# Sums of token blocks for the last two groups: operands read from PSUM on VectorE, and the places of their splits

## The chip, the cores and the metric

One core of a Trainium2 chip runs the whole program. The metric is the device time of one execution in microseconds; before the change it was 810.95 us, the median of 3 runs (809.65 to 811.36).

## The reference

Eight batches of 576 tokens pass through an attention layer (8 heads of width 64; heads 0 to 3 see a local window of 32 positions, heads 4 to 7 a stride of 32) and then through a mixer layer. All is float32:

```python
scores = np.where(masks[None], scale * np.matmul(q, k.transpose(0, 1, 3, 2)), -1e9)
x = softmax(scores) @ v                       # as [batch, 576, 512]
h = np.maximum(xt @ w_tok1, 0.0) @ w_tok2     # xt = x transposed to [batch, 512, 576]
u = x + h.transpose(0, 2, 1)
h2 = np.maximum(u @ w_ch1, 0.0) @ w_ch2       # w_ch1 512 x 1536, w_ch2 1536 x 512
return u + h2
```

The change lies in the last step, `u @ w_ch1`, for the last 1024 of the 4608 tokens.

## The kernel before

**Numbers.** Every float32 operand of a large product is held as two parts, a high part rounded to the format that TensorE multiplies (`fp32r`) and a low part, the rest: `uh`/`ul`, `w1h`/`w1l`, `gh`/`gl`. A product is three matmuls (high·high, high·low, low·high). A *split* makes the two parts of a tile: a copy on ScalarE (ACT) gives the high part, a subtraction on VectorE (DVE) the low one.

**Groups.** The 4608 tokens form nine groups of 512 (`GT`), 0 to 8. `u` of a group is eight tiles of 128 x 512, high and low for four blocks `cc` of 128 channels. A batch's 576 tokens fill the rest of one group and a part of the next: `tok2` (L483) makes them, first the 64 tokens of batch 7 that end group 7 (a narrow call), then the 512 tokens that are group 8. It transposes `x` into a PSUM tile `pu`, adds `h·w_tok2` there, copies `uh` from it on ACT (L516) and subtracts on DVE (L517). It is called for two `cc` at a time, and its two PSUM tiles come from a pool `ps_t` of two banks.

**Groups 0 to 6** go through `mlp` (L909). It walks over 12 blocks of 128 hidden channels: an up product (L921), ReLU and split (L926, L927), a down product that adds to four accumulators (`down`, L712). Between these are numbered slots, four to a block, into which other work is put by hand with `at(slot, function)`. All engines follow the order in which the program is written (`manual_schedule`), so an instruction that waits holds everything behind it on its own engine. In group 6 (L1099 to L1113) slots 35 and 36 hold the two narrow calls for batch 7, slots 37 and 39 the two calls that make group 8. Slot 38 lies inside the down product of block 9, slots 39 and 40 directly behind it; then come the down products of blocks 10 and 11, 24 matmuls.

**Groups 7 and 8** go together through `last_two` (L794), which replaces the eight block products of a 2 x 2 by 2 x 2 product by seven (Strassen's scheme as Winograd wrote it). The weights are taken as 2 x 2 blocks of 128 x 256, the tokens as two halves of channels by two groups. With `b1` = group 7 and `b2` = group 8, four sums of token blocks are needed, each of two tiles of 128 x 512 and each split:

- t1 = b2[0:2] − b1[0:2]
- t2 = b2[2:4] − t1
- t3 = b2[2:4] − b2[0:2]
- t4 = b1[2:4] − t2

`token_sums` (L748) makes them as a generator whose parts are run at slots 38 and 40 and then three times in the first iteration of `last_two`. `chain` (L722) applies one operation after the other to one output tile. Since `b1` and `b2` are read as high and low parts, t1 takes three operations a tile, t2 two, t3 three (on GpSimd, POOL), t4 two (one tile on DVE, one on POOL). The tile `third` that holds t3 has the name `sw`, of which there is one buffer.

`weight_sums(i)` (L731) makes the four sums of weight blocks s1 to s4 of iteration `i`: ten operations of 128 x 256 on POOL into the tile `sw`, then four splits (L743 on ACT, L744 on DVE) into tiles `sh`, `sl`. Those of iterations 0 and 1 are made in group 6.

**The loop of `last_two`** has six iterations of two hidden blocks. `times` (L802) is one of the seven products, six matmuls. The order of iteration 0 on TensorE (PE) is a11·b11, a12·b21, s1·t1, s2·t2, s4·b22, s3·t3. The order of a later iteration is s1·t1, a11·b11, then a22·t4 of the iteration before (`last_product`), a down product of 12 matmuls, s4·b22, s2·t2, a down product, s3·t3, a12·b21. `kept` (L820) copies a PSUM tile to SBUF on ACT; `plus` (L825) adds a PSUM tile and an SBUF tile on DVE; `relu` (L805, L806) is ReLU with a split.

- The product s2·t2 adds to the bank `a` of a11·b11, and so waits until `kept(a)` has copied it (`p1`).
- The product s3·t3 adds to the same bank, and so waits until `kept(a)` has copied it again (`p16`).
- The first product of iteration i + 1 writes the bank `h0`, and so waits until `c12 = plus(b, p16)` has read it.

`result` (L705) adds `u` to an accumulator (L708 on DVE; for group 6 L709 on POOL) and stores it. For group 6 blocks 0 and 1 are done behind the last down product, blocks 2 and 3 at the end of iteration 0.

Of the kernel before, what the change touches and what calls it, by code (L numbers as in the profile page):

```python
# [10 lines left out]
F32 = mybir.dt.float32  # L11
# [12 lines left out]
DM = H * D  # L24
# [83 lines left out]
def attn_mixer_kernel(ctx, tc, qT, kT, vw, qs, ks, vs, qsT, ksT, vsP, mask, words, outT):  # L108
# [374 lines left out]
    def tok2(ps_t, x_t, h, us, b, tail, ccs, whole_t2=None):  # L483

        t0, t1 = _span(b, tail)
        n, g0 = t1 - t0, 0 if tail else 64 * b
        o = 0 if t0 else 64
        chunks = [*([] if t0 else [NSC - 1]), *range(max(t0 - 64, 0) // P, (t1 - 64) // P)]
        pus = [ps_t.tile() for _ in ccs]
        for pu, cc in zip(pus, ccs):  # L490
            cs = slice(P * cc, P * cc + P)
            for k, c in enumerate(chunks):
                ps_t.matmul(pu[:, P * k:P * k + P], x_t[:, c, cs], ident,
                                 is_transpose=True, start=(k == 0), stop=False, skip_group_check=True)
        narrow = whole_t2 is None and n <= NARROW
        for pu, cc in zip(pus, ccs):
            cs = slice(P * cc, P * cc + P)
            if narrow:
                sides = pu[:, o:o + 2 * n].rearrange("p (k n) -> p k n", k=2)
            pu = pu[:, o:o + n]  # L500
            for m in range(2):
                if whole_t2 is not None:
                    terms = ((pu, h[m], whole_t2[:, m]),)
                else:
                    hh, hl = h[m]
                    th, tl, both = t2h[:, m, t0:t1], t2l[:, m, t0:t1], t2[:, m, :, t0:t1]
# [221 lines left out]

    combos = {}

    def weight_sums(i):  # L731

        a11, a12, a21, a22 = ([w[:, 2 * c:2 * c + 2, P * f:P * f + P].bitcast(F32) for w in (w1h, w1l)] for f in (2 * i, 2 * i + 1) for c in range(2))
        whole = pools["fin"].tile([P, 4, 2, P], F32, name="sw")
        s1, s2, s3, s4 = (whole[:, k] for k in range(4))
        chain(nc.gpsimd, s1, a21[0], (ALU.add, a22[0]), (ALU.add, a21[1]), (ALU.add, a22[1]))
        chain(nc.gpsimd, s2, s1, (ALU.subtract, a11[0]), (ALU.subtract, a11[1]))
        chain(nc.gpsimd, s3, a11[0], (ALU.subtract, a21[0]), (ALU.add, a11[1]), (ALU.subtract, a21[1]))
        chain(nc.gpsimd, s4, a12[0], (ALU.subtract, s2), (ALU.add, a12[1]))
        yield  # L740
        sh, sl = (pools["fin"].tile([P, 4, 2, P], F32R, name="s" + k, bufs=2) for k in "hl")
        for k in range(4):
            nc.scalar.copy(out=sh[:, k], in_=whole[:, k])  # L743
            nc.vector.tensor_tensor(out=sl[:, k], in0=whole[:, k], in1=sh[:, k].bitcast(F32), op=ALU.subtract)  # L744
        combos[i] = [(sh[:, k], sl[:, k]) for k in range(4)]
        yield

    def token_sums():  # L748

        def f(pair):  # L750
            return [t.bitcast(F32) for t in pair]

        b1, b2 = us[NG - 2], us[NG - 1]
        t1 = [const.tile([P, NSC, DT], F32R, name="t1" + k).rearrange("p c n -> p (c n)")[:, :2 * GT].rearrange("p (c n) -> p c n", c=2) for k in "hl"]
        wholes = []
        for c in range(2):
            x, y = f(b2[c]), f(b1[c])
            w = xp.tile([P, GT], F32, name="xh")
            chain(nc.vector, w, x[0], (ALU.subtract, y[0]), (ALU.add, x[1]), (ALU.subtract, y[1]))
            wholes.append(w)  # L760
        todo = [split_u(w, t1[0][:, c], t1[1][:, c]) for c, w in enumerate(wholes)]
        yield
        for g in todo:
            g()
        t2 = xp.tile([P, NSC, DM], F32R, name="x", bufs=1).rearrange("p c n -> p (c n)")[:, :4 * GT].rearrange("p (k c n) -> p k c n", k=2, c=2)
        twos = []
        for c in range(2):
            x = f(b2[2 + c])
            w = xp.tile([P, GT], F32, name="xlo")
            chain(nc.vector, w, x[0], (ALU.subtract, wholes[c]), (ALU.add, x[1]))  # L770
            twos.append(w)
        third = pools["fin"].tile([P, 4, 2, P], F32, name="sw").rearrange("p (c k) m n -> p c (k m n)", c=2)
        for c in range(2):
            x, y = f(b2[2 + c]), f(b2[c])
            chain(nc.gpsimd, third[:, c], x[0], (ALU.subtract, y[0]), (ALU.add, x[1]), (ALU.subtract, y[1]))
        for g in [split_u(w, t2[:, 0, c], t2[:, 1, c]) for c, w in enumerate(twos)]:
            g()
        t3 = [[xp.tile([P, DM], F32R, name=f"h{k}{m}", bufs=1) for m in range(2)] for k in "hl"]
        t4 = const.tile([P, 2, 2, S], F32R, name="t2").rearrange("p c k n -> p (c k n)")[:, :4 * GT].rearrange("p (k c n) -> p k c n", k=2, c=2)
# [6 lines left out]
        for c in range(2):  # L786
            x = f(b1[2 + c])
            chain((nc.vector, nc.gpsimd)[c], twos[c], x[0], (ALU.subtract, twos[c]), (ALU.add, x[1]))
        yield
        for g in [split_u(w, t4[:, 0, c], t4[:, 1, c]) for c, w in enumerate(twos)]:  # L790
            g()
        yield

    def last_two():  # L794
# [45 lines left out]
        for i in range(NFC // 2):  # L840
# [5 lines left out]
            if i:  # L846
# [2 lines left out]
                times(a, a11, b11, True)  # L849
                p5, p1 = kept(b), kept(a)  # L850
                last_product(i - 1, before)
                down_all(fe - 2)
                times(b, s4, b22, False)
                times(a, s2, t2, False)
            else:
                times(a, a11, b11, True)
                p1 = kept(a, "gh")
                times(c, a12, b21, True)
                t1, t2, t3, t4 = combos["t"]
                times(b, s1, t1, True)  # L860
# [5 lines left out]
            c12 = plus(b, p16)  # L866
            if i:
                down_all(fo - 2)
            else:
                next(combos["token"])  # L870
            if i:
                next(sums, None)
                sums = weight_sums(i + 2) if i + 2 < NFC // 2 else iter(())
                next(sums, None)
            times(a, s3, t3, False)
            later[fo] = plus(a, p5)
            if i:
                times(c, a12, b21, True)
            else:
                next(combos["token"])  # L880
            hidden[fe] = relu(plus(c, p1, None if i else "gl"), *new_g())
            later[fe] = relu(flat(c12), *in_place(fe))
            if i == 0:
                sums = weight_sums(2)
                next(sums)
                while left:
                    left.pop(0)()
            combos["a22"], before = a22, a
# [93 lines left out]
    def do_tok2(b, tail, ccs=range(NCC)):  # L982
        g = b + tail
        if g not in us:
            us[g] = new_u(pools["fin"] if g == NG - 1 else up if g % 2 else xp)
        tok2(ps_t, state["x"], state["h"], us[g], b, tail, ccs, None if b else t2e)

    def opened(name, **how):
        closing[name] = tc.tile_pool(name=name, reuse_waits="tile", **how)
# [86 lines left out]
    for g in range(NG - 2):  # L1076
# [10 lines left out]
        if b < B:  # L1087
# [11 lines left out]
            if b == B - 1:  # L1099
                at(21, attention_ends)  # L1100
                made["sums"] = []
                for i, k in ((21, 0), (26, 0), (26, 1), (31, 1)):
                    at(i, lambda i=i, k=k: (made["sums"].append(weight_sums(k)) if len(made["sums"]) == k else None, next(made["sums"][k])))
                for i, t in enumerate((37, 39)):
                    at(t, lambda i=i: do_tok2(b, True, (2 * i, 2 * i + 1)))

                def token_begins():
                    combos["token"] = token_sums()
                    next(combos["token"])

# [144 lines left out]
```

## Time and profile before

| | us |
|---|---|
| median of 3 runs (lowest, highest) | 810.95 (809.65, 811.36) |
| the profiled execution | 811.38 |
| its span in the profile | 809.6 |
| TensorE busy | 783.3 |
| VectorE busy | 530.4 |
| GpSimd busy | 319.7 |
| ScalarE busy | 259.8 |

The profile is of one execution; times in it count from the start of its span. PE is TensorE's matmuls, DVE VectorE, ACT ScalarE, POOL GpSimd. A busy time says how long instructions ran, not that the engine worked at its best: the duration of a matmul counts from its start to the end of its results, while the next one starts before that. The granted clock is a share of TensorE's full speed of 2.4 GHz; 0.5 is its lower level of 1.2 GHz. In a timeline a row gives start, duration, engine, line, operation, output and inputs, and how many were merged; brackets hold the engine's idle time ahead of it and what ended that.

### The profile page before, as it was taken

What the parts mean: (1) busy time and instruction counts of PE and PEld (TensorE: products, weight loads), DVE (VectorE), ACT (ScalarE), POOL (GpSimd) and SP (SyncE); (2) the same over time, 40 slices, a digit from 0 to 9 for tenths busy, and PEclk for the clock granted to TensorE, in tenths of its full rate; (3) what the DMA queues carried; (4) which work ended last, traced back from release to release, by engine and by line L of the source; (5) the groups of instructions that cost most, each with busy time, mean ns of one, the idle gap of its engine ahead of it and who ended that gap; (6) DMA issues with size and microseconds to landing.
All of it is one profiled execution on the core that took longest, in us unless ns stands there. A gap on an engine that the chain in (4) does not pass through costs nothing.

```text
span 809.6 us, 16277 instructions
## 1 busy us (share of the span) xinstructions
PE 783.3 (97%) x6284; PEld 639.7 (79%) x6284; DVE 530.4 (66%) x1810; ACT 259.8 (32%) x611; POOL 319.7 (39%) x330
## 2 busy tenths in 40 slices
PE   6799999999999999999999999999999998899997
PEld 5567778888888878888888888888888886688886
DVE  4687985556467777766767678677786459654340
ACT  6577873233222222222212222222121322333300
POOL 2300000043105782279127932685267607853000
PEclk9899999999999999999999999999999999999999
DMA  9547782245504250335033321434021200000011
GB/s 355 177 135 247 239 270 72 92 153 157 145 1 161 76 148 3 111 101 152 23 109 103 94 82 40 128 89 130 7 77 48 57 1 27 26 1 1 0 66 39
DMA packets 61545, 79.82 MB, mean 99 GB/s; under 512 B 16316, under 2 KB 46908, under 8 KB 61468
## 3 DMA queue, kind: packets, MB, share of 16 engines
q1 hardware_dynamic: 60044, 74.32, 29.6%
q0 software_dynamic: 1136, 4.06, 1.4%
q8 instruction: 49, 0.80, 0.4%
q10 hardware_dynamic: 288, 0.40, 0.1%
q14 instruction: 28, 0.23, 0.1%
HBM read 60.16 MB, written 18.48 MB: 97 GB/s over the span
## 4 chain that ended last, share of the span: by engine, by line
PE 84%; DVE 7%; ACT 4%; DMA 3%; issue 1%; SPq 0%; ACTq 0%; DVEq 0%
PE acc L716 29%; PE h L921 25%; PE t L82 19%; PE t L802 3%; PE h L802 2%; PE h L716 2%; PE t L716 2%; DVE xlo L726 1%; ACT as L185 1%; PE t L85 1%; DMA x<-xs 1%; DMA ek<-in_ksT 1%; ACT w_raw L138 1%; PE h L85 1%; DMA mask_sb<-in_mask 1%
## 5 line engine op out<-in xcount | busy, mean ns | idle before, releaser
L414 POOL TENSOR_TENSOR sprod<-sv,ss 128x512 f32<-128x512 f32 (+9 forms) x150 | 136.2, 951 | 122.1 <-issue 52.5
L366 POOL TENSOR_TENSOR sprod<-sk,sq 128x512 f32<-128x512 f32 x80 | 102.2, 1307 | 136.7 <-DVE ss L367 97.2
L716 PE MATMUL acc<-gh,w2h 128*128 128x512 f32 x384 | 152.3, 397 | 0.5 <-ACT gh L805 0.5
L716 PE MATMUL acc<-gl,w2h 128*128 128x512 f32 x384 | 150.4, 392 | 0.2 <-DVE gl L806 0.2
L716 PE MATMUL acc<-gh,w2l 128*128 128x512 f32 x384 | 150.4, 392 | 0.0
L921 PE MATMUL h<-uh,w1h 128*128 128x512 f32 x336 | 134.5, 400 | 2.1 <-DVE ul L517 1.4
L921 PE MATMUL h<-uh,w1l 128*128 128x512 f32 x336 | 131.3, 391 | 0.0
L921 PE MATMUL h<-ul,w1h 128*128 128x512 f32 x336 | 131.0, 390 | 0.0
L927 DVE SCALAR_TENSOR_TENSOR gl<-h,gh 128x512 fp32r<-128x512 f32 x84 | 57.8, 688 | 59.6 <-ACT gh L926 59.4
L926 ACT ACTIVATE gh<-h 128x512 fp32r<-128x512 f32 x84 | 50.5, 601 | 111.2 <-PE h L921 111.2
L416 DVE TENSOR_REDUCE so<-sprod 128x64 f32<-128x512 f32 (+9 forms) x150 | 73.9, 526 | 17.8 <-POOL sprod L414 17.7
L716 PEld LDWEIGHTS acc<-gh,w2l 128*128 128x128 f32 x384 | 72.5, 189 | 15.6
L716 PEld LDWEIGHTS acc<-gh,w2h 128*128 128x128 f32 x384 | 72.4, 189 | 15.4 <-ACT gh L805 1.0
L716 PEld LDWEIGHTS acc<-gl,w2h 128*128 128x128 f32 x384 | 72.6, 189 | 14.7 <-DVE gl L806 0.5
L185 ACT ACTIVATE as<-as,am 128x64 f32<-128x64 f32 x216 | 55.8, 337 | 67.4 <-DVE am L182 67.4
L921 PEld LDWEIGHTS h<-uh,w1h 128*128 128x128 f32 x336 | 63.1, 188 | 16.8 <-DVE ul L517 2.2
L921 PEld LDWEIGHTS h<-uh,w1l 128*128 128x128 f32 x336 | 63.1, 188 | 13.6
L921 PEld LDWEIGHTS h<-ul,w1h 128*128 128x128 f32 x336 | 63.2, 188 | 12.0
L182 DVE CUSTOM_DVE_ANT_0 as<-t,mask_sb 128x64 f32<-128x64 f32 x216 | 34.1, 220 | 33.0 <-PE t L82 26.8
L367 DVE TENSOR_REDUCE ss<-sprod 128x8 f32<-128x512 f32 x80 | 51.2, 670 | 6.2 <-POOL sprod L366 6.0
L517 DVE TENSOR_TENSOR ul<-t,uh 128x512 fp32r<-128x512 f32 (+5 forms) x44 | 22.9, 526 | 39.8 <-ACT uh L516 39.7
L82 PE MATMUL t<-t,hh 128*128 128x384 f32 (+5 forms) x184 | 47.9, 342 | 0.0
(198 smaller groups left out, 1238.7 us busy)
## 6 DMA issues: line engine op xcount, KB each, us to landing
w_raw<-in_words SPq DMA_DIRECT2D x21, 512.0 KB
lv<-in_vw SPq DMA_DIRECT2D x18, 390.0 KB
out_t<-xh SPq DMA_DIRECT2D x20, 256.0 KB
out_t<-xlo SPq DMA_DIRECT2D x16, 256.0 KB
lk<-in_kT SPq DMA_DIRECT2D x18, 208.0 KB
x<-xl SPq DMA_DIRECT2D x14, 256.0 KB
lq<-in_qT SPq DMA_DIRECT2D x18, 192.0 KB
xl<-ax SPq DMA_DIRECT2D x18, 192.0 KB
```

Of the source, the lines that this page charges most:

```text
L82: self.tc.stamp_issue_order_token(self.tc.nc.tensor.matmul(*args, **how).ins, self.pool.name)
L182: nc.vector.tensor_tensor_reduce(out=s_t[:, c, j, :], in0=sc[j].of[:, 64 * c:64 * c + 64], in1=mask_sb[:, m, :], scale=-SCALE, scalar=TOP, ...
L185: nc.scalar.activation(out=s_t[:, c, j, :], in_=s_t[:, c, j, :], func=AF.Exp, bias=m_t[:, c, j:j + 1], scale=-1.0)
L366: nc.gpsimd.tensor_tensor(out=pr, in0=k_t[:, n0:n0 + n], in1=q_t[:, i:i + 1].to_broadcast([P, n, D]), op=ALU.mult)
L367: return [lambda: nc.vector.tensor_reduce(out=s_t[:, i, n0:n0 + n], in_=pr, axis=AX.X, op=ALU.add)]
L414: nc.gpsimd.tensor_tensor(out=pr, in0=v_t[:, d0:d1, :n], in1=s_t[:, n - 1:n, :n].to_broadcast([P, d1 - d0, n]), op=ALU.mult)
L416: todo.append(lambda n=n, d0=d0, d1=d1, pr=pr: nc.vector.tensor_reduce(out=o_t[:, n - 1, d0:d1], in_=pr, axis=AX.X, op=ALU.add))
L716: nc.tensor.matmul(acc[cc], l[:, fc, cs], r, start=(fc == 0 and k == 0), stop=(fc == NFC - 1 and k == 2))
L802: nc.tensor.matmul(bank, a[x][:, c], b[c][y], start=start and c == 0 and k == 0, stop=(c == 1 and k == 2), skip_group_check=True)
L921: nc.tensor.matmul(ph, l[:, cc, fs], r, start=(cc == 0 and k == 0), stop=(cc == NCC - 1 and k == 2))
L926: nc.scalar.activation(out=gh, in_=ph, func=AF.Relu)
L927: nc.vector.scalar_tensor_tensor(out=gl, in0=ph, scalar=0.0, in1=gh.bitcast(F32), op0=ALU.max, op1=ALU.subtract)
```

## The change

1. `token_sums` begins at slot 36, with four new additions on POOL, high + low of each of the four tiles of group 7, into `wholes`. `tok2` returns its PSUM tiles, and `token_sums` takes them: behind the call at slot 37 it makes t1 as `pus - wholes` (one operation a tile), behind the call at slot 39 t2 as `pus - t1` (one) and t3 as `pus - b2h - b2l` (two), all on DVE. Slot 38 has t1's low parts, slot 40 those of t2 and then t4 as `wholes - t2` (one operation a tile, on DVE).
2. In iteration 0 the split of t3 follows the copy `p1`, and that of t4 the copy `p5`; nothing of `token_sums` comes later.
3. `weight_sums(2)` no longer runs on POOL from the end of iteration 0 on; it is made as a whole in iteration 1, behind `last_product(0)`, with its ten operations on DVE and its splits right behind them. `weight_sums(3)` and later ones stay on POOL, where they were.

```diff
-    def weight_sums(i):
+    def weight_sums(i, engine=nc.gpsimd):
...
-        chain(nc.gpsimd, s1, a21[0], (ALU.add, a22[0]), (ALU.add, a21[1]), (ALU.add, a22[1]))
+        chain(engine, s1, a21[0], (ALU.add, a22[0]), (ALU.add, a21[1]), (ALU.add, a22[1]))
...
     def token_sums():
-        b1, b2 = us[NG - 2], us[NG - 1]
+        b1 = us[NG - 2]
+        wholes = []
+        for c in range(NCC):
+            wholes.append(xp.tile([P, GT], F32, name="xh" if c < 2 else "xlo"))
+            nc.gpsimd.tensor_tensor(out=wholes[c], in0=b1[c][0].bitcast(F32), in1=b1[c][1].bitcast(F32), op=ALU.add)
+        pus = yield
+        b2 = us[NG - 1]
...
-        wholes = []
         for c in range(2):
-            x, y = f(b2[c]), f(b1[c])
-            w = xp.tile([P, GT], F32, name="xh")
-            chain(nc.vector, w, x[0], (ALU.subtract, y[0]), (ALU.add, x[1]), (ALU.subtract, y[1]))
-            wholes.append(w)
-        todo = [split_u(w, t1[0][:, c], t1[1][:, c]) for c, w in enumerate(wholes)]
+            nc.vector.tensor_tensor(out=wholes[c], in0=pus[c], in1=wholes[c], op=ALU.subtract)
+        todo = [split_u(wholes[c], t1[0][:, c], t1[1][:, c]) for c in range(2)]
         yield
         for g in todo:
             g()
+        pus = yield
...
-            chain(nc.vector, w, x[0], (ALU.subtract, wholes[c]), (ALU.add, x[1]))
...
-            chain(nc.gpsimd, third[:, c], x[0], (ALU.subtract, y[0]), (ALU.add, x[1]), (ALU.subtract, y[1]))
+            nc.vector.tensor_tensor(out=wholes[c], in0=pus[c], in1=wholes[c], op=ALU.subtract)
+        for c in range(2):
+            chain(nc.vector, third[:, c], pus[c], (ALU.subtract, b2[c][0]), (ALU.subtract, b2[c][1]))
+        todo = [split_u(wholes[c], t2[:, 0, c], t2[:, 1, c]) for c in range(2)]
+        yield
+        for g in todo:
+            g()
+        for c in range(2):
+            nc.vector.tensor_tensor(out=wholes[2 + c], in0=wholes[2 + c], in1=wholes[c], op=ALU.subtract)
...
-        for c in range(2):
-            x = f(b1[2 + c])
-            chain((nc.vector, nc.gpsimd)[c], twos[c], x[0], (ALU.subtract, twos[c]), (ALU.add, x[1]))
-        yield
-        for g in [split_u(w, t4[:, 0, c], t4[:, 1, c]) for c, w in enumerate(twos)]:
+        for g in [split_u(wholes[2 + c], t4[:, 0, c], t4[:, 1, c]) for c in range(2)]:
             g()
         yield
...
                 last_product(i - 1, before)
+                if i == 1:
+                    for _ in weight_sums(2, nc.vector):
+                        pass
                 down_all(fe - 2)
...
                 times(a, a11, b11, True)
                 p1 = kept(a, "gh")
+                next(combos["token"])
                 times(c, a12, b21, True)
...
                 down_all(fo - 2)
-            else:
-                next(combos["token"])
-            if i:
-                next(sums, None)
+                if i > 1:
+                    next(sums, None)
                 sums = weight_sums(i + 2) if i + 2 < NFC // 2 else iter(())
                 next(sums, None)
             times(a, s3, t3, False)
...
             if i:
                 times(c, a12, b21, True)
-            else:
-                next(combos["token"])
...
             if i == 0:
-                sums = weight_sums(2)
-                next(sums)
                 while left:
                     left.pop(0)()
...
-                for i, t in enumerate((37, 39)):
-                    at(t, lambda i=i: do_tok2(b, True, (2 * i, 2 * i + 1)))
...
-                at(38, token_begins)
-                for t in (40,):
-                    at(t, lambda: next(combos["token"]))
+                at(36, token_begins)
+                for i, t in enumerate((37, 39)):
+                    at(t, lambda i=i: combos["token"].send(do_tok2(b, True, (2 * i, 2 * i + 1))))
+                    at(t + 1, lambda: next(combos["token"]))
```

## Rows read from the trace of the kernel before

**Rows 1.** The page's head and its part 1: busy time, share of span, instructions.

```profile
span 809.6 us, 16277 instructions
...
PE 783.3 (97%) x6284; PEld 639.7 (79%) x6284; DVE 530.4 (66%) x1810; ACT 259.8 (32%) x611; POOL 319.7 (39%) x330
```

**Rows 2.** Windows: length, busy time and count of each engine, granted clock, DMA share, GB/s.

```profile
650.00:673.72 23.72, 23.64 (x124) 19.75 (x123) 13.52 (x24) 5.96 (x13) 4.20 (x3) 1.00 0.00 1
673.72:710.10 36.38, 30.75 (x121) 23.12 (x120) 28.49 (x32) 12.13 (x24) 29.63 (x28) 0.95 0.08 30
693.81:697.84 4.03, 4.03 (x12) 3.23 (x12) 3.72 (x5) 1.72 (x4) 3.79 (x5) 0.63 0.00 0
710.10:780.00 69.90, 69.90 (x310) 57.91 (x309) 29.33 (x46) 19.28 (x40) 17.77 (x23) 1.00 0.00 1
```

**Rows 3.** Timeline of PE: start, duration, what; its idle time before in brackets.

```profile
664.67 1.03 PE L82 MATMUL t<-ident,x 128*128 128x128 f32 x8
...
668.05 0.39 PE L82 MATMUL t<-t,hl 128*128 128x512 f32 x1
...
673.72 0.39 PE L802 MATMUL t<-uh,w1h 128*128 128x512 f32 x1
...
677.57 0.39 PE L802 MATMUL h<-t1h,sl 128*128 128x512 f32 x1
680.87 0.73 PE L802 MATMUL t<-x,sh 128*128 128x512 f32 x2 [2.91 <-ACT gh L820]
```

**Rows 4.** Waits of PE from 650 us on: total us, times, longest.

```profile
PE t L802 <- ACT gh L820: 2.9, 1, 2.9
PE t L802 <- DVE t L720: 1.0, 2, 0.8
```

**Rows 5.** Chain that ended last, in order of time: start, us, what.

```profile
700.74 2.72 PE acc L716 x12
```

**Rows 6.** Timeline of DVE, 655 to 703 us.

```profile
655.46 0.22 DVE L517 TENSOR_TENSOR ul<-xlo,uh 128x64 fp32r<-128x64 f32 x1 [0.31 <-ACT uh L516]
...
662.76 0.69 DVE L517 TENSOR_TENSOR ul<-t,uh 128x512 fp32r<-128x512 f32 x1 [0.67 <-ACT uh L516]
...
664.68 1.42 DVE L726 TENSOR_TENSOR xh<-xh,ul 128x512 f32<-128x512 f32 x2
...
669.32 1.29 DVE L517 TENSOR_TENSOR ul<-t,uh 128x512 fp32r<-128x512 f32 x2 [1.17 <-ACT uh L516]
...
674.64 1.66 DVE L726 TENSOR_TENSOR xlo<-xlo,ul 128x512 f32<-128x512 f32 x1
...
682.17 3.11 DVE L720 TENSOR_TENSOR hl<-sw,hh 128x512 fp32r<-128x512 f32 x2
685.21 0.68 DVE L825 TENSOR_TENSOR ul<-h,uh 128x512 f32<-128x512 f32 x1
...
693.67 1.22 DVE L806 SCALAR_TENSOR_TENSOR w1l<-ul,w1h 128x512 fp32r<-128x512 f32 x1
...
702.01 1.42 DVE L744 TENSOR_TENSOR sl<-sw,sh 128x256 fp32r<-128x256 f32 x4
```

**Rows 7.** Timeline of ACT.

```profile
679.71 0.62 ACT L719 CAST x<-xlo 128x512 fp32r<-128x512 f32 x1 [2.69 <-DVE xlo L726]
...
701.26 1.33 ACT L743 CAST sh<-sw 128x256 fp32r<-128x256 f32 x4
```

**Rows 8.** Timeline of POOL.

```profile
681.74 3.00 POOL L709 TENSOR_TENSOR xh<-xh,ul 128x512 f32<-128x512 f32 x2 [2.60 <-DVE xh L708]
684.70 1.73 POOL L726 TENSOR_TENSOR xlo<-uh,xlo 128x512 f32<-128x512 f32 x1
...
698.09 2.53 POOL L709 TENSOR_TENSOR xh<-xh,ul 128x512 f32<-128x512 f32 x2
703.51 0.74 POOL L726 TENSOR_TENSOR sw<-w1h 128x256 f32<-128x256 f32 x1 [2.89 <-DVE sl L744]
```

**Rows 9.** Window of the first two stores of group 6: same columns as rows 2.

```profile
683.06:687.00 3.94, 3.39 (x15) 2.29 (x14) 3.91 (x4) 0.09 (x1) 3.86 (x3) 1.00 0.35 133
```

More of the change, by code (lines that the diff above doesn't have):

```diff
@@ L517, in tok2 @@
             nc.vector.tensor_tensor(out=ul, in0=whole, in1=uh.bitcast(F32), op=ALU.subtract)
+        return pus
     closing = {"late": tc.tile_pool(name="late", bufs=1, side="right")}
@@ L735, in weight_sums @@
         s1, s2, s3, s4 = (whole[:, k] for k in range(4))
-        chain(nc.gpsimd, s1, a21[0], (ALU.add, a22[0]), (ALU.add, a21[1]), (ALU.add, a22[1]))
-        chain(nc.gpsimd, s2, s1, (ALU.subtract, a11[0]), (ALU.subtract, a11[1]))
-        chain(nc.gpsimd, s3, a11[0], (ALU.subtract, a21[0]), (ALU.add, a11[1]), (ALU.subtract, a21[1]))
-        chain(nc.gpsimd, s4, a12[0], (ALU.subtract, s2), (ALU.add, a12[1]))
+        chain(engine, s1, a21[0], (ALU.add, a22[0]), (ALU.add, a21[1]), (ALU.add, a22[1]))
+        chain(engine, s2, s1, (ALU.subtract, a11[0]), (ALU.subtract, a11[1]))
+        chain(engine, s3, a11[0], (ALU.subtract, a21[0]), (ALU.add, a11[1]), (ALU.subtract, a21[1]))
+        chain(engine, s4, a12[0], (ALU.subtract, s2), (ALU.add, a12[1]))
         yield
@@ L748, in token_sums @@
     def token_sums():
-        def f(pair):
-            return [t.bitcast(F32) for t in pair]
-        b1, b2 = us[NG - 2], us[NG - 1]
+        b1 = us[NG - 2]
[5 more added lines that the diff above has]
+        b2 = us[NG - 1]
         t1 = [const.tile([P, NSC, DT], F32R, name="t1" + k).rearrange("p c n -> p (c n)")[:, :2 * GT].rearrange("p (c n) -> p c n", c=2) for k in "hl"]
-        wholes = []
         for c in range(2):
-            x, y = f(b2[c]), f(b1[c])
-            w = xp.tile([P, GT], F32, name="xh")
-            chain(nc.vector, w, x[0], (ALU.subtract, y[0]), (ALU.add, x[1]), (ALU.subtract, y[1]))
-            wholes.append(w)
-        todo = [split_u(w, t1[0][:, c], t1[1][:, c]) for c, w in enumerate(wholes)]
+            nc.vector.tensor_tensor(out=wholes[c], in0=pus[c], in1=wholes[c], op=ALU.subtract)
+        todo = [split_u(wholes[c], t1[0][:, c], t1[1][:, c]) for c in range(2)]
         yield
@@ L764, in token_sums @@
             g()
+        pus = yield
         t2 = xp.tile([P, NSC, DM], F32R, name="x", bufs=1).rearrange("p c n -> p (c n)")[:, :4 * GT].rearrange("p (k c n) -> p k c n", k=2, c=2)
-        twos = []
-        for c in range(2):
-            x = f(b2[2 + c])
-            w = xp.tile([P, GT], F32, name="xlo")
-            chain(nc.vector, w, x[0], (ALU.subtract, wholes[c]), (ALU.add, x[1]))
-            twos.append(w)
+        t3 = [[xp.tile([P, DM], F32R, name=f"h{k}{m}", bufs=1) for m in range(2)] for k in "hl"]
+        t4 = const.tile([P, 2, 2, S], F32R, name="t2").rearrange("p c k n -> p (c k n)")[:, :4 * GT].rearrange("p (k c n) -> p k c n", k=2, c=2)
         third = pools["fin"].tile([P, 4, 2, P], F32, name="sw").rearrange("p (c k) m n -> p c (k m n)", c=2)
         for c in range(2):
-            x, y = f(b2[2 + c]), f(b2[c])
-            chain(nc.gpsimd, third[:, c], x[0], (ALU.subtract, y[0]), (ALU.add, x[1]), (ALU.subtract, y[1]))
-        for g in [split_u(w, t2[:, 0, c], t2[:, 1, c]) for c, w in enumerate(twos)]:
-            g()
-        t3 = [[xp.tile([P, DM], F32R, name=f"h{k}{m}", bufs=1) for m in range(2)] for k in "hl"]
-        t4 = const.tile([P, 2, 2, S], F32R, name="t2").rearrange("p c k n -> p (c k n)")[:, :4 * GT].rearrange("p (k c n) -> p k c n", k=2, c=2)
+            nc.vector.tensor_tensor(out=wholes[c], in0=pus[c], in1=wholes[c], op=ALU.subtract)
[4 more added lines that the diff above has]
+        for g in todo:
+            g()
+        for c in range(2):
+            nc.vector.tensor_tensor(out=wholes[2 + c], in0=wholes[2 + c], in1=wholes[c], op=ALU.subtract)
         combos["t"] = [[(h[:, c], l[:, c]) for c in range(2)] for h, l in (t1, (t2[:, 0], t2[:, 1]))]
@@ L785, in token_sums @@
         yield
-        for c in range(2):
-            x = f(b1[2 + c])
-            chain((nc.vector, nc.gpsimd)[c], twos[c], x[0], (ALU.subtract, twos[c]), (ALU.add, x[1]))
-        yield
-        for g in [split_u(w, t4[:, 0, c], t4[:, 1, c]) for c, w in enumerate(twos)]:
+        for g in [split_u(wholes[2 + c], t4[:, 0, c], t4[:, 1, c]) for c in range(2)]:
             g()
@@ L985, in do_tok2 @@
             us[g] = new_u(pools["fin"] if g == NG - 1 else up if g % 2 else xp)
-        tok2(ps_t, state["x"], state["h"], us[g], b, tail, ccs, None if b else t2e)
+        return tok2(ps_t, state["x"], state["h"], us[g], b, tail, ccs, None if b else t2e)
     def opened(name, **how):
```

## The prediction, made before the changed kernel was run

> **What bounds the kernel now.** The page first: TensorE is busy 783.3 of 809.6 us [rows 1], so only its gaps can be won. The windows say where they are: full until 673.72 us, where `last_two` begins, and from 710.10 on; between, 30.75 busy of 36.38 us [rows 2]. The program has 120 matmuls in that stretch (36 in iteration 0, 66 in iteration 1, 18 of iteration 2 up to its first down product). Twelve take 2.72 us at full pace [rows 5], or 0.2267 each, so 120 want 27.20 us. **9.18 us are lost there**, and that is the most the change can win.
>
> The waits of PE name the causes [rows 4]. The largest is at s2·t2: PE stands from 677.8 to 680.87 [rows 3], released by the copy `p1`. That copy was ready long before; it stood on ACT behind the high copy of t2 (679.71 [rows 7]), which waited for the DVE chain of t2. The next waits are t3, t4 and the ReLU of the first hidden block, all late from the same DVE queue. Last, the 12 matmuls from 693.81 on took 4.03 us at a granted clock of 0.63, part of it at the lower level of 1.2 GHz [rows 2]: 1.31 us over 2.72.
>
> Why DVE is late is in the durations. Alone, an operation of 128 x 512 takes 0.68 us, two independent ones 1.29, two dependent ones 1.42; with both inputs in SBUF beside POOL it takes 1.66, and a pair 3.11 [rows 6]. POOL worked on t3, on t4 and on the weight sums at that time. First what rows show: at 685.21 a DVE addition that reads one operand from PSUM took 0.68 [rows 6] inside a POOL operation of 684.70 to 686.43 [rows 8]. So I price operations with a PSUM operand at 0.645 always, and those with two SBUF operands so only while POOL is idle. The Trainium skill (SBUF — State Buffer, Who interferes with whom) states this as a rule: a VectorE instruction with two SBUF inputs contends with a GpSimd instruction that reads SBUF, and the later one blocks for the whole of the other. The trace agrees, by the 0.68 beside the 1.66. The rule speaks against one part of the change, the weight sums on DVE.
>
> **Slots 36 to 38.** POOL gets four additions, 1.27 each alone (2.53 for two [rows 8]), 1.73 when blocked: 5.1 to 6.9 us. The inputs of the first two are there by 655.7 [rows 6], so t1's operands are ready by about 659, those of t4 by 662. DVE, behind the second `ul` (662.76 + 0.69 [rows 6]), makes t1 in two operations, to 664.75, where it used six. This wait on POOL is new; behind it stand the last `gl` of group 6, t1's low parts and the next `ul`, none wanted before 671. PE wants the two PSUM banks back at 664.67 [rows 3] and four transposes later (about 665.2); they come free at 664.1 and 664.75. Cost: nothing, with 0.4 us in hand.
>
> **Slots 39 and 40.** `tok2` ends at 668.44 (668.05 + 0.39 [rows 3]). ACT copies at once, since t1's copies are done by then: 669.06. In DVE's order: last `ul` to 669.75; t2, two of 0.645, to 671.04; t3, two dependent pairs (2 x 1.355), to 673.75; t2's low parts to 675.04; t4 to 676.33. The bank that a11·b11 wants at 673.72 is free at 671.7, after the first operation of t3. All this lies beside 24 down matmuls.
>
> **Iteration 0.** On a PE without gaps s2·t2 is due at 673.72 + 18 x 0.2267 = 677.80, s3·t3 at 680.52, the first product of iteration 1 at 681.88. t2 is there at 675.04 and `p1`, now behind no late copy, at 675.9: the 3.07 us go. DVE then does the two L708 of group 6 (677.62), and these start POOL's two L709. t3's low parts have both inputs in SBUF and meet them; I take the pair's 3.11 [rows 6], which was taken beside the same L709 (681.74 [rows 8]): 680.73. The first is there by 679.2 and the second is wanted at 681.4. t4's low parts: 682.02. `c12`: 682.70, where PE wants its bank at 681.88: **a wait of 0.8 us stays**. Alone, the pair would take 1.29 and nothing would wait: bounds 0 and 0.8; I take 0.8, since L709 is released just there. Then two additions, ACT's ReLU (0.62, as its other 128 x 512 writes [rows 7]) and `gl` (0.69) put the first hidden block at 685.4; the down product wants it at 682.70 + 18 x 0.2267 = 686.78. t4 is wanted at 685.4. The waits there go.
>
> The group-6 stores on SP's queue come about 5 us earlier. Blocks 2 and 3 need the buffers of the first two, at about 686. The first two stores took 3.94 us from the first issue to the last byte [rows 9]: 0.52 MB at 133 GB/s. The second would be issued at about 680.7, so they are through by 684.6, with 1.4 us in hand.
>
> **Weight sums of iteration 1, on DVE.** DVE's queue behind `last_product(0)`: L708 twice to 687.9, `gl` 688.6, the strided `w1l` 1.22 [rows 6] to 689.8. Ten operations of 128 x 256 are new. DVE's four subtractions of that shape took 1.42, or 0.355 each [rows 6]; the 512-wide dependent ones took 0.065 more than independent ones, so seven at 0.42 and three at 0.355 make 4.0, to 693.8. POOL took 0.74 for one [rows 8], 7.4 for ten; I keep that as the upper end. On ACT the last high copy (four took 1.33 [rows 7]) follows at about 694.2, and **behind it in ACT's order stands `p16`**, 694.8. PE wants `p16` for s3·t3 at 686.78 + 36 x 0.2267 = 694.94. Bounds: no wait at 4.0, 3.3 us at 7.4. One blocked start costs about 0.5; I take 0.3. On POOL these ten are saved (7.4 us and more), hidden before and after. `weight_sums(3)` starts when DVE is done with `sw`, at about 695 for 703.51 [rows 8], as much earlier as PE is.
>
> **Clock.** Both waits left are under 1 us, so I take the 1.31 us of the low clock as won; 3.07 us of standing did not lower it at once either, it fell only after the third group of waits. The Trainium skill (TensorE: Matmul & The Clock Gate, HAM oscillation) tells of kernels that pay the transition again and again because of their gaps; by that a dip might come back, at 804.2.
>
> **Sum.** 9.18 − 0.8 − 0.3 = 8.1 us off. The profiled execution took 811.38, 0.43 over the median and at the upper edge of the runs; it goes to 803.3, the median to 802.85, say **802.9**.
>
> **Rivals.**
>
> 1. *The wait moves to iteration 1.* DVE with its ten sums and ACT with `p16` behind them hold s3·t3. At 0.74 each the median is 810.95 − 9.18 + 0.8 + 3.3 = 805.9; if each also waited for a POOL operation (0.355 + 0.74, 11 us), 7 us: 809.6. Against: after L709 ends, near 690, POOL has no work until DVE is through. For: the margin is 0.14 us. Chance 0.13.
> 2. *Reading PSUM is no cheaper.* If the new operations on `pus` took the 1.2 to 1.7 of before, eight of them would add 4 to 8 us to DVE's queue and make `c12` later by as much: 802.9 + 4 to 802.9 + 8, 806.9 to 810.9, no change at the upper end. Against: `ul` reads PSUM in 0.69 [rows 6]. Chance 0.04; the changed kernel would then not do what it is written to do, since VectorE would still set the pace.
> 3. *Slower: the banks of `tok2` wait for POOL.* The bank for slot 39 now comes free only when t1 has read it, and t1 waits for POOL's first addition. For each microsecond that this ends after 663.5, less 0.5, PE stands one more, ahead of everything else. It turns slower when it ends after about 672.5, 17 us after its inputs; at 676 the time would be 814.5. Against: POOL ran only three instructions between 650 and 673.72 [rows 2]. For: its tile is one that the attention path used shortly before. Chance 0.03.
>
> The forecast has the remaining 0.80: from 801.0 (all 9.18 won, 801.8, less 0.8 for the scatter of the runs, whose lowest is 1.3 under the median) to 804.5. Taking in most of the first rival, the range is **801.0 to 806.0**. A measurement of this kernel tells about 0.2% (1.6 us) from no change. Faster by more takes the forecast and nearly all of the first rival, with half of the second: 0.94. Within 0.2%: 0.03. Slower: 0.03.
>
> **What would show it.** PE's gap before s2·t2 and the waits on t3 and t4 are gone; 120 matmuls from the first product on take about 28.3 us; one wait of PE below 1 us on `c12` (L825) at the start of iteration 1, a small one or none on `p16` (L820); DVE's 128 x 512 subtractions near 0.65; no clock below 1.00 after 670. Wrong would be: a wait on L820 of 2 us or more at s3·t3 of iteration 1, a gap of PE between 662 and 673, or a duration over 1 us for a subtraction that reads PSUM.

## The result and the profile after

The changed kernel takes **802.66 us**, the median of 4 runs (802.29 to 802.93). Before, it was 811.13 us, the median of 4 runs (809.65 to 811.36; one run more than the 810.95 at the head is the median of). The ratio is 0.9899, 95% interval 0.9882 to 0.9916: 8.5 us or 1.0% off, where 802.9 was forecast.

The head of the page of the changed kernel and its busy times, for [rows 1]:

```profile
span 800.2 us, 16271 instructions
...
PE 780.3 (98%) x6284; PEld 639.0 (80%) x6284; DVE 528.1 (66%) x1818; ACT 260.5 (33%) x611; POOL 303.3 (38%) x316
```

The windows answer to [rows 2]; their columns are length, busy time and count of each engine, granted clock, DMA share, GB/s. The first one covers the 24 down matmuls behind slot 39 and what stands ahead of them, the second the 120 matmuls from the first product of `last_two` to the first down product of iteration 2.

```profile
664.00:672.78 8.78, 8.78 (x44) 7.37 (x42) 7.13 (x12) 3.21 (x6) 0.00 (x0) 1.00 0.00 0
672.78:700.76 27.98, 27.82 (x121) 22.36 (x120) 24.17 (x38) 11.39 (x22) 11.58 (x12) 1.00 0.10 38
```

**The 120 matmuls now take 27.98 us for 36.38**, at full clock, with PE idle for 0.16. The change took 8.40 us from that stretch. The other 1.0 us between the two profiled spans lies elsewhere: `last_two` begins at 672.78 instead of 673.72, and 0.93 us are there already at slot 35, behind code that is the same (the first reduction of `tok2` on DVE starts at 653.19 for 654.12). Executions differ in that part: in the profiles below `last_two` begins between 672 and 678 us (at 681.46 with the late addition). So small effects are read from the length of this stretch, which I call **the stretch**; its floor is 120 x 0.2267 = 27.20. It is read from one execution of each kernel.

The waits of PE from 640 us on are this one row, for [rows 4]:

```profile
PE h L797 <- DVE ul L820: 0.2, 1, 0.2
```

PE's timeline, for [rows 3]: the second wide `tok2` call, s2·t2, the first product of iteration 1, and s3·t3 of iteration 1.

```profile
663.73 1.03 PE L82 MATMUL t<-ident,x 128*128 128x128 f32 x8
...
676.86 0.61 PE L797 MATMUL t<-x,sh 128*128 128x512 f32 x2
...
681.26 0.50 PE L797 MATMUL h<-t1h,sh 128*128 128x512 f32 x1 [0.16 <-DVE ul L820]
...
693.81 0.50 PE L797 MATMUL t<-hh,sh 128*128 128x512 f32 x1
```

s2·t2 follows without a gap, where it stood for 2.91 us. Of the 0.78 us above the floor, 0.43 go at 681.26 (the wait on `c12`, then a slower restart) and 0.24 at 693.81.

DVE's timeline, for [rows 6]: a narrow `ul`, t1 from PSUM, one tile of t3, the low parts of t2, t3 and t4, `c12`, and the weight sums of iteration 2 (first and last of ten).

```profile
654.53 0.98 DVE L517 TENSOR_TENSOR ul<-xlo,uh 128x64 fp32r<-128x64 f32 x1 [0.31 <-ACT uh L516]
...
662.44 1.28 DVE L759 TENSOR_TENSOR xh<-t,xh 128x512 f32<-128x512 f32 x2
...
669.97 0.68 DVE L727 TENSOR_TENSOR sw<-t,uh 128x512 f32<-128x512 f32 x1
670.68 0.69 DVE L727 TENSOR_TENSOR sw<-sw,ul 128x512 f32<-128x512 f32 x1
...
672.62 1.28 DVE L721 TENSOR_TENSOR x<-xh,x 128x512 fp32r<-128x512 f32 x2
...
676.22 3.17 DVE L721 TENSOR_TENSOR hl<-sw,hh 128x512 fp32r<-128x512 f32 x2
679.32 1.28 DVE L721 TENSOR_TENSOR t<-xlo,t 128x512 fp32r<-128x512 f32 x2
680.52 0.68 DVE L820 TENSOR_TENSOR ul<-h,uh 128x512 f32<-128x512 f32 x1
...
688.53 0.41 DVE L727 TENSOR_TENSOR sw<-w1h 128x256 f32<-128x256 f32 x1
...
692.41 0.42 DVE L727 TENSOR_TENSOR sw<-sw,w1l 128x256 f32<-128x256 f32 x1
```

`p16` on ACT, for which s3·t3 waits at 693.81:

```profile
693.18 0.58 ACT L815 COPY uh<-t 128x512 f32<-128x512 f32 x1
```

POOL's timeline, for [rows 8]: the first and last of its four additions, and the two pairs of L709 (now L710).

```profile
654.15 1.28 POOL L754 TENSOR_TENSOR xh<-uh,ul 128x512 f32<-128x512 f32 x1 [9.80 <-DVE ul L517]
...
658.53 1.30 POOL L754 TENSOR_TENSOR xlo<-uh,ul 128x512 f32<-128x512 f32 x1 [0.16 <-DVE ul L517]
675.85 3.00 POOL L710 TENSOR_TENSOR xh<-xh,ul 128x512 f32<-128x512 f32 x2 [16.03 <-DVE xh L709]
685.51 2.55 POOL L710 TENSOR_TENSOR xh<-xh,ul 128x512 f32<-128x512 f32 x2 [6.66 <-DVE xh L709]
```

A subtraction of 128 x 512 that reads PSUM takes 0.64 to 0.68 us, and one from SBUF while POOL stands idle 0.64 to 0.69. Of these subtractions only t3's low parts, beside the L710 at 675.85, still take 3.17.

### The profile page after: what moved, and what is told of

Read it like the earlier page. It is cut to its first block, busy times and chain, and to the rows that moved or that the text cites. A ratio compares the mean times of both kernels' runs of the same rounds, so it can differ in the third digit from the quotient of the medians.

```text
span 800.2 us, 16271 instructions
## 1 busy us (share of the span) xinstructions
PE 780.3 (98%) x6284; PEld 639.0 (80%) x6284; DVE 528.1 (66%) x1818; ACT 260.5 (33%) x611; POOL 303.3 (38%) x316
## 4 chain that ended last, share of the span: by engine, by line
PE 85%; DVE 6%; ACT 4%; DMA 2%; issue 1%; POOL 1%; SPq 0%; ACTq 0%; DVEq 0%; POOLq 0%
PE acc L717 28%; PE h L914 25%; PE t L82 19%; PE t L797 4%; PE h L797 3%; PE h L717 2%; PE t L717 2%; DMA w_raw<-in_words 2%; ACT as L185 1%; PE t L85 1%; POOL sprod L366 1%; ACT w_raw L138 1%; DVE xlo L450 1%; DMA mask_sb<-in_mask 1%; DVE gl L920 1%
```

## The experiments

The engines' lines shift a little from kernel to kernel; names are those of the program. "Before" beside each was run on the same chip in turn with it, since that median moved between 809.55 and 810.17.

### Part 3 alone, on the kernel before

```diff
...
+                if i == 1:
+                    for _ in weight_sums(2, nc.vector):
+                        pass
...
-                sums = weight_sums(2)
-                next(sums)
```

> The kernel before with part 3 alone: weight_sums(2) on DVE in iteration 1, everything else as before. Theory (the gain is DVE's shorter queue of token sums, three operations a tile turned into one, and POOL off t3 and t4): the waits at s2·t2 (3.07 us) and at t3 (0.71 us) stand before the moved sums and stay. What goes is POOL's company beside the low parts of t4 (2.40 us for the pair would become about 1.3), with at most the 1.31 us of the low clock: 1 to 2.4 us faster than before, ratio to before 0.997 to 0.999. Rival (it was mainly POOL's weight sums that slowed DVE, and moving them is most of the gain): 5 us or more, ratio 0.994 or less.

810.30 us, before 809.79; ratio 1.0009 (0.9998 to 1.002). The stretch, and a part of it in which the clock was low:

```profile
675.67:710.94 35.27, 30.42 (x122) 23.27 (x120) 31.54 (x42) 12.44 (x24) 20.57 (x18) 0.95 0.08 30
684.20:687.50 3.30, 3.30 (x9) 2.58 (x8) 3.00 (x3) 0.69 (x2) 3.30 (x3) 0.52 0.25 87
```

The low parts of t4 on DVE, here and then in the kernel before, with POOL beside them there:

```profile
691.29 1.29 DVE L720 TENSOR_TENSOR t<-xlo,t 128x512 fp32r<-128x512 f32 x2
```

```profile
689.36 2.40 DVE L720 TENSOR_TENSOR t<-xlo,t 128x512 fp32r<-128x512 f32 x2
...
689.35 1.87 POOL L726 TENSOR_TENSOR sw<-sw,w1l 128x256 f32<-128x256 f32 x2
```

The pair takes 1.29 for 2.40, and the stretch is 1.1 us shorter in this profile; the runs show nothing of it. The wait at s2·t2 stays at 2.91 us, as the theory had it. The one at t3 does not show, against the theory: the clock fell behind s2·t2, PE reached s3·t3 late, and t3 was there. A new wait of 1.07 us comes, on `p16` in iteration 1. **The rival falls: moving the weight sums is not the gain.** The gain of 1 us or more that I had forecast was not seen either, so the time is a miss.

### Part 3 undone, in the changed kernel

```diff
-                if i == 1:
-                    for _ in weight_sums(2, nc.vector):
-                        pass
...
             if i == 0:
+                sums = weight_sums(2)
+                next(sums)
```

> The changed kernel with part 3 undone: weight_sums(2) on POOL again from the end of iteration 0, its splits in iteration 1 where they were. Theory: POOL can begin only when t3's split has read the tile sw, near 679.4 us, and then works beside the low parts of t4 (two SBUF inputs): the pair takes 2.4 to 3.1 us for 1.28, c12 is 1.1 to 1.8 us later, and PE's wait of 0.3 at the start of iteration 1 becomes 1.4 to 2.1; the wait of 0.13 on p16 goes. 803.7 to 804.3 us. Rival (weight sums off POOL are most of the gain): 807 us or more.

801.71 us, before 809.79; ratio 0.9903 (0.9879 to 0.9926), beside 0.9899 for the whole change. The stretch, t4's low parts on DVE, and the first POOL sum beside them:

```profile
674.17:702.35 28.18, 27.49 (x121) 22.45 (x120) 20.69 (x28) 11.09 (x22) 20.36 (x22) 1.00 0.10 38
```

```profile
680.70 1.82 DVE L721 TENSOR_TENSOR t<-xlo,t 128x512 fp32r<-128x512 f32 x2
```

```profile
681.21 0.77 POOL L727 TENSOR_TENSOR sw<-w1h 128x256 f32<-128x256 f32 x1 [0.98 <-DVE hl L721]
```

The stretch is 0.2 us longer: 0.5 more at `c12`, none on `p16`. The time is below the 803.7 to 804.3 expected. The pair took 1.82, not 2.4 to 3.1. I had priced it from the 2.40 of the kernel before, beside two POOL operations of 128 x 256, and from the 3.11 beside two of 128 x 512; here it waited for a single one of 0.77. So part 3 carries nothing that the runs can tell.

### Operands in SBUF again

```diff
-            nc.vector.tensor_tensor(out=wholes[c], in0=pus[c], in1=wholes[c], op=ALU.subtract)
+            chain(nc.vector, wholes[c], b2[c][0].bitcast(F32), (ALU.subtract, wholes[c]), (ALU.add, b2[c][1]))
```

and likewise t2 (from `b2[2 + c]`) and t3 (three operations a tile), all on DVE.

> The changed kernel with its places and engines, but t1, t2 and t3 made from the high and low parts of group 8 in SBUF instead of PSUM: two, two and three operations a tile for one, one and two, six more on DVE. Theory (the number of operations in DVE's queue is what counts): six at about 0.7 us, of which some 0.7 us fall into DVE's idle time before slot 39, so c12 is about 3.5 us later and PE waits 3.4 us more at the start of iteration 1: 806.0 us, up to 807.3 if the clock falls. Rival (what counted was POOL beside DVE, and POOL is idle here): within 0.5 us of the changed kernel, 802.2 to 803.2.

807.97 us, before 809.79; ratio 0.9974 (0.9963 to 0.9985). The stretch, the part with a low clock, and two of PE's waits:

```profile
671.96:704.54 32.58, 29.79 (x121) 23.35 (x120) 25.92 (x43) 11.89 (x22) 12.26 (x13) 0.95 0.09 33
683.91:687.04 3.13, 3.12 (x7) 2.48 (x8) 2.44 (x5) 1.31 (x3) 0.00 (x0) 0.51 0.00 0
```

```profile
PE t L797 <- DVE hl L721: 1.5, 2, 0.8
PE h L797 <- DVE ul L820: 1.1, 1, 1.1
```

Six operations more on DVE's queue make the stretch 4.6 us longer. They came not only at `c12`, as forecast, but also at t3's low parts, and the clock fell behind them (3.13 us at 0.51, some 1.5 of the 4.6). With POOL idle beside these sums, **more than half of the gain is gone: the number of operations counts.** The rival falls; the time is 0.7 us over the top of what was expected.

### All sums on DVE, in the kernel before

```diff
-            chain(nc.gpsimd, third[:, c], x[0], (ALU.subtract, y[0]), (ALU.add, x[1]), (ALU.subtract, y[1]))
+            chain(nc.vector, third[:, c], x[0], (ALU.subtract, y[0]), (ALU.add, x[1]), (ALU.subtract, y[1]))
...
-            chain((nc.vector, nc.gpsimd)[c], twos[c], x[0], (ALU.subtract, twos[c]), (ALU.add, x[1]))
+            chain(nc.vector, twos[c], x[0], (ALU.subtract, twos[c]), (ALU.add, x[1]))
```

with t3 put behind the low parts of t2.

> The kernel before with t3 and the second tile of t4 on DVE too, t3 behind the low parts of t2, so that POOL stands idle beside the token sums; all sums still from the parts in SBUF, eight operations more on DVE. Theory (to keep POOL away is worth only part of it; with three operations a tile DVE's queue alone is too long): t2 is there near 676 and the first wait of 3.07 us goes, but t3's low parts end at 682.6 to 684.4, 2 to 3 us late, and those of t4 near 690, another 2 to 3 us late; the 120 matmuls from the first product on take 32.5 to 35.5 us, for 36.38 before and 27.98 in the changed kernel. Rival (POOL beside DVE was nearly all of it): 31 us or less.

809.47 us, before 809.55; ratio 0.9999 (0.9987 to 1.001). The stretch, and on DVE the low parts of t2, t3 and t4:

```profile
673.27:708.49 35.22, 31.52 (x122) 23.20 (x121) 28.00 (x38) 12.02 (x24) 22.30 (x22) 0.95 0.08 30
```

```profile
673.92 1.47 DVE L720 TENSOR_TENSOR x<-xlo,x 128x512 fp32r<-128x512 f32 x2
...
680.61 3.13 DVE L720 TENSOR_TENSOR hl<-sw,hh 128x512 fp32r<-128x512 f32 x2
...
689.12 1.81 DVE L720 TENSOR_TENSOR t<-xlo,t 128x512 fp32r<-128x512 f32 x2
```

t2 is there at 675.4 and the wait of 2.9 us is gone. But t3's low parts end at 683.74, where they ended at 685.28 [rows 6], and t4's at 690.93; the stretch is 35.22. **To take t3 and t4 off POOL without shortening DVE's queue brings next to nothing.** POOL was not idle beside all of the sums, as I had meant it to be: its weight sums begin at 683.89, and the low parts of t4 beside them take 1.81 for 1.28. So this run does not part the two causes. What each is worth in the changed kernel is read from the run above, where the longer queue alone costs 4.6 us, and from the next, where POOL is back beside a short queue.

### t3 on POOL, in the changed kernel

```diff
-            chain(nc.vector, third[:, c], pus[c], (ALU.subtract, b2[c][0]), (ALU.subtract, b2[c][1]))
+            chain(nc.gpsimd, third[:, c], b2[2 + c][0].bitcast(F32), (ALU.subtract, b2[c][0]), (ALU.add, b2[2 + c][1]), (ALU.subtract, b2[c][1]))
```

> The changed kernel with t3 made on POOL from the parts in SBUF, three operations a tile, as in the kernel before; DVE has four operations fewer. Theory (POOL beside DVE, and ACT's order behind a late t3, cost more than the four operations): POOL takes 1.6 us for each of six, t3 is there near 678.5, its high copies hold p5, t4's copies and p16 on ACT, and s3·t3 waits 2.3 to 3.5 us; the 120 matmuls take 30.3 to 32.8 us. Rival (DVE's number of operations alone counts): c12 comes 2.7 us earlier, 27.6 us or less.

804.21 us, before 810.17; ratio 0.9925 (0.9907 to 0.9942). The stretch; t2's low parts and t4 on DVE; the first operation of t3 on POOL; PE's wait for `c12`:

```profile
672.64:701.78 29.14, 27.80 (x122) 22.37 (x121) 25.09 (x37) 11.50 (x22) 14.81 (x14) 1.00 0.10 37
```

```profile
670.04 2.99 DVE L721 TENSOR_TENSOR x<-xh,x 128x512 fp32r<-128x512 f32 x2
672.95 3.48 DVE L778 TENSOR_TENSOR xlo<-xlo,xh 128x512 f32<-128x512 f32 x2
```

```profile
666.74 1.29 POOL L727 TENSOR_TENSOR sw<-uh 128x512 f32<-128x512 f32 x1 [7.09 <-ACT uh L516]
```

```profile
682.57 0.50 PE L797 MATMUL h<-t1h,sh 128*128 128x512 f32 x1 [1.07 <-DVE ul L820]
```

DVE has four operations fewer and is nevertheless later: the two pairs with both inputs in SBUF take 2.99 and 3.48 for 1.28 each. PE waits 1.07 at `c12` and the stretch grows by 1.2 us. The rival falls. My own size was too large, and the path was another: s3·t3, where I had expected 2.3 to 3.5 us, waits 0.27. POOL began at 666.74, when only the high parts were there, and took 1.3 us an operation while DVE read PSUM, so ACT's copies were hardly held. With POOL beside a short queue, 7.2 of the 8.4 us of the change remain.

### Part 2 undone: the splits at their old places

```diff
                 p1 = kept(a, "gh")
-                next(combos["token"])
...
             if i:
                 times(c, a12, b21, True)
+            else:
+                next(combos["token"])
```

> The changed kernel with part 2 undone: the split of t3 behind the copy p5, that of t4 behind the second addition of iteration 0, as in the kernel before. Theory (what was late was the sums, not their splits): t3's low parts then meet POOL's L709 only at the first of the two and are there when s3·t3 wants them, c12 no longer stands behind the low parts of t4 and PE's wait of 0.32 us for it goes, t4 and the first hidden block are there by 0.3 us. The 120 matmuls from the first product on take 27.6 to 28.0 us, for 27.98 in the changed kernel; no difference that the median can tell. Rival (the early places of the splits are what removed the waits on t3 and t4): these waits come back, 1 to 2.7 us, 803.5 to 805.5.

803.91 us, before 810.17; ratio 0.9913 (0.9894 to 0.9932). The stretch; on DVE t3's low parts and the first weight sum; on PE s3·t3 of iteration 1:

```profile
673.59:702.60 29.01, 27.63 (x121) 22.29 (x120) 23.01 (x38) 11.20 (x22) 11.55 (x12) 1.00 0.10 37
```

```profile
679.01 1.35 DVE L721 TENSOR_TENSOR hl<-sw,hh 128x512 fp32r<-128x512 f32 x2 [1.89 <-ACT hh L720]
...
689.30 1.50 DVE L727 TENSOR_TENSOR sw<-w1h 128x256 f32<-128x256 f32 x1
```

```profile
695.67 0.50 PE L797 MATMUL t<-hh,sh 128*128 128x512 f32 x1 [1.38 <-ACT uh L815]
```

The waits on t3 and t4 do not come back, so the rival falls; t3's low parts even escape L709, with 1.35, and the wait on `c12` is gone, as expected. But the low parts of t4 now stand ahead of the first hidden block; L708 and L709 of blocks 2 and 3 come 1.2 us later and meet the weight sums, whose first operation takes 1.50 for 0.41. `p16` is late by 1.4 us. The stretch is 29.01 for the 27.6 to 28.0 expected, a miss; the time lies in the rival's 803.5 to 805.5, but through this other wait.

### Weight sums on POOL at the same place

```diff
-                    for _ in weight_sums(2, nc.vector):
+                    for _ in weight_sums(2, nc.gpsimd):
```

> The changed kernel with weight_sums(2) at the same place in iteration 1 but on POOL. Theory (ACT's high copies of these sums stand ahead of p16, for which s3·t3 waits): POOL begins near 688.1 us and takes 7.4 to 7.7, the last high copy ends near 696.1 and p16 near 696.7, where s3·t3 is due at 693.7: PE's wait there grows from 0.13 to about 3.0, 805.5 us. Rival (the sums are wanted only in iteration 2, and have the time): no change, 802.2 to 803.2.

808.04 us, before 809.79; ratio 0.9978 (0.9961 to 0.9994). The stretch and the part with a low clock; on ACT the last high copy of the sums and `p16` behind it; on PE s3·t3:

```profile
677.79:710.96 33.17, 29.43 (x122) 23.51 (x120) 20.68 (x28) 11.39 (x22) 21.34 (x24) 0.95 0.09 32
703.70:707.08 3.38, 3.38 (x9) 2.64 (x8) 0.85 (x2) 0.00 (x0) 3.14 (x5) 0.51 0.00 0
```

```profile
701.47 0.40 ACT L744 CAST sh<-sw 128x256 fp32r<-128x256 f32 x1 [1.14 <-POOL sw L727]
701.78 0.58 ACT L815 COPY uh<-t 128x512 f32<-128x512 f32 x1
```

```profile
702.41 0.50 PE L797 MATMUL t<-hh,sh 128*128 128x512 f32 x1 [3.60 <-ACT uh L815]
```

**The sums are wanted only in iteration 2, but PE stands 3.6 us for them in iteration 1**, since `p16` is behind their copies on ACT. The theory holds; the time is 2.5 us over the 805.5 expected: the wait was 0.6 longer, and 3.38 us at a clock of 0.51 came behind it, some 1.7 us.

### POOL's first addition twelve times

```diff
-            nc.gpsimd.tensor_tensor(out=wholes[c], in0=b1[c][0].bitcast(F32), in1=b1[c][1].bitcast(F32), op=ALU.add)
+            for _ in range(1 if c else 12):
+                nc.gpsimd.tensor_tensor(out=wholes[c], in0=b1[c][0].bitcast(F32), in1=b1[c][1].bitcast(F32), op=ALU.add)
```

> The changed kernel with POOL's first addition done twelve times over (the same result), so that t1's first operand is there near 669.7 us instead of 655.4. Theory (slot 39 of tok2 can't have its PSUM banks back until t1 has read them): PE stands ahead of the second wide tok2 call for about 6.4 us, from 663.7 to 670.1; nothing behind it changes its order, so the whole is 6 to 8 us slower, with the clock, 808.5 to 810.5. Rival (the banks are free when the splits of u have read them, t1 may come later): less than 2 us slower.

812.34 us, before 810.17; ratio 1.0022 (1.0011 to 1.0034). The part behind the wait and the stretch; the second wide `tok2` call on PE (the profile names no releaser); t1's first operation on DVE:

```profile
670.00:674.00 4.00, 3.40 (x12) 2.77 (x13) 2.29 (x5) 1.73 (x3) 3.27 (x3) 0.50 0.00 0
681.46:709.17 27.71, 27.55 (x122) 22.38 (x120) 23.89 (x38) 11.40 (x22) 11.59 (x12) 1.00 0.10 38
```

```profile
670.41 1.09 PE L82 MATMUL t<-ident,x 128*128 128x128 f32 x4 [7.24 <-issue]
```

```profile
669.62 0.69 DVE L760 TENSOR_TENSOR xh<-t,xh 128x512 f32<-128x512 f32 x1 [7.81 <-POOL xh L755]
```

PE begins 0.1 us after t1 has read the bank: 7.2 us of standing and then about 4 us at the low level of 1.2 GHz. The stretch behind it is as good as ever. The third rival of the prediction is real: 9.7 us above the changed kernel's 802.66, where 6 to 8 were expected.

### Both remaining waits taken away

```diff
-        (nc.gpsimd if grp == NG - 3 else nc.vector).tensor_tensor(out=o_t, in0=o_t, in1=ul.bitcast(F32), op=ALU.add)
+        nc.vector.tensor_tensor(out=o_t, in0=o_t, in1=ul.bitcast(F32), op=ALU.add)
...
-                    for _ in weight_sums(2, nc.vector):
-                        pass
+                    sums = weight_sums(2, nc.vector)
+                    next(sums)
...
-                if i > 1:
-                    next(sums, None)
+                next(sums, None)
```

> The changed kernel with both of its remaining waits taken away: the splits of weight_sums(2) stand behind the second down product of iteration 1, so that p16 no longer stands behind them on ACT, and L709 of group 6 runs on DVE, so that t3's low parts meet no POOL operation. Theory (the two waits are ACT's order and the blocked pair): no gap over 0.1 us, the 120 matmuls take 27.2 to 27.4 us for 27.98, about 0.7 us off, which the median can hardly tell. Rival (PE's restarts there come from elsewhere): 27.9 us or more.

802.41 us, before 810.17; ratio 0.9898 (0.988 to 0.9917). The stretch, and t3's low parts:

```profile
673.75:700.99 27.24, 27.24 (x121) 22.46 (x120) 23.54 (x42) 11.09 (x22) 5.12 (x6) 1.00 0.11 39
```

```profile
678.65 1.28 DVE L721 TENSOR_TENSOR hl<-sw,hh 128x512 fp32r<-128x512 f32 x2
```

The stretch is at its floor, 27.24 for 27.20, with no wait of PE left. So the two named causes were all that the changed kernel still lost there. In the median the 0.7 us can't be told from the changed kernel, as expected.

## Why the prediction was right

- **The time.** 802.66 for 802.9 is closer than the runs allow, and in part luck. The median of the kernel before lay at 811.13 beside the changed kernel, and at 809.55 to 810.17 in the later sets of 15 to 29 runs; against those the gain would be 6.9 to 7.5 us instead of 8.5. The changed kernel was not timed again beside them. The waits and the stretch say more than this agreement.
- **What bounds it.** 9.18 us were to be won in the stretch; 8.40 were, and the experiment without the remaining waits reaches 9.14. That the rest of the time is PE at full pace held.
- **s2·t2 and `p1`.** The 2.9 us are gone: t2's low parts end 1.1 us after the first product began (673.90 less 672.78), 1.3 forecast.
- **The price of an operation on PSUM**, 0.645: measured 1.28 for two at every place, and they start 0.60 apart. I took two for 1.29 each time and so counted the tail of each pair twice. This is the one term that was sized wrongly in DVE's ledger: by `c12` the queue was 0.56 us ahead of it (8.42 us after the first product began, for 8.98).
- **The wait on `c12`**, 0.8 forecast within 0 to 0.8: 0.43 with the restart. The blocked pair of t3's low parts was forecast at 3.11 and took 3.17; the error is the term above.
- **`p16` behind the weight sums**, 0.3 forecast within 0 to 3.3: 0.24. Ten sums took 4.3 us (688.53 to 692.83) for 4.0. I had put the 0.3 down to one blocked start; the first of the sums was not blocked (0.41), but the ReLU's low part ahead of it took 1.66 for the 1.22 of the forecast. That the size came out is in part luck. The upper end, with POOL's price, was tried: 3.6 us.
- **The stores of group 6** hold nothing: the L708 of blocks 2 and 3 begin at 684.41, with no gap on DVE ahead of them.
- **POOL's additions at slot 36**: about 1.3 each and all done by 659.83; t1 began at 662.44. What I had left out is that they block the narrow `ul` of DVE, 0.98 for 0.22 [rows 6]; it cost nothing.
- **The clock.** It stayed at 1.00 in the whole stretch, so its 1.31 us came back, as I took it. A dip such as the Trainium skill tells of (TensorE: Matmul & The Clock Gate, HAM oscillation) did not come in this stretch; one came in each of the runs above that stood longer. That the standing at s2·t2 did not lower the clock at once was so in the trace before, but is no rule: in part 3 alone the same 2.91 us were followed, 1.4 us later, by 3.30 us at 0.52.
- **Which part does it.** The prediction let the gain come from shorter queues in part 1 and put a price, not a gain, on part 3. The experiments bear that out: part 3 alone does nothing that can be measured, and without parts 2 or 3 most of the gain stays (0.9913 and 0.9903). Taken back in part 1, the operands alone give back 4.6 of 8.4 us, and t3 on POOL 1.2, with four operations fewer on DVE. So the shorter queue is the larger cause. The rest was not parted further, and part 1 was not run by itself.
- **The rivals.** The first shows where the sums cost POOL's price (808.04). The second is refuted by the 0.68 of t3 from PSUM; it counted eight operations on `pus`, but two of them, the second ones of t3, read only SBUF (0.69 with POOL idle). The third was forecast to turn slower when the first addition ends after about 672.5 (672.1 by its own rule, and 814.9 for its 814.5). With the late addition it ended near 669.6, which is 671.2 in the times of the trace before, where the matmul ahead of the call starts at 664.43 for 662.79. By the rule that is 7.2 us of standing, as measured, and 810.1 us; it was 812.34, because I had left out that the clock falls behind the standing, some 2 us.

## What to carry to other kernels

Look at an engine's queue as a ledger: number of operations, the price of each with its neighbour running, and the time at which the result is due. Read a sum's operand where it is whole, in PSUM, ahead of its split: it saves the operations that put the parts together again, and in these traces it also kept VectorE clear of GpSimd. The bank is then free only when the sum has read it: with the late addition that cost 7.2 us of standing. Where work is moved to fill a gap, ask what stands behind its last instruction on each engine that it uses, not only when its result is wanted.

## What the runs showed that I had not expected

The granted clock fell to about 0.5 for 3 to 4 us in the profiles in which PE had stood for 2.9 us (part 3 alone), 2.8 (operands in SBUF), 3.6 (sums on POOL) and 2.1 (all sums on DVE) in the stretch so far, and for 7.2 with the late addition. It did not where PE's waits there were 0.2 to 1.4 us. A stretch of 3.30 us at 0.52 holds about 1.6 us less work than one at full clock, so each of these waits cost 1.5 to 2 us more than it shows, and in the expectations I had left that out or taken it too low. One wait does not settle it: in the kernel before the clock stayed at 1.00 behind the same 2.91 us and fell only 13 us later, behind several short waits. No run shows what makes the difference.

GpSimd operations of 128 x 256 beside VectorE cost less than those of 128 x 512: the blocked pair took 1.82 beside one of them (part 3 undone) and 2.40 beside two (the kernel before), against 3.17 beside two of 128 x 512. That is what the Trainium skill's rule of blocking for the whole of the other instruction would make of it (SBUF — State Buffer, Who interferes with whom): in part 3 undone one short operation was waited for, of 0.77, instead of two long ones.
